# Window attention with channel mix on one core: a new order of 1054 steps, new buffer slots, and 33 steps on other engines

## The chip, the cores and the metric

The kernel runs on one core of a Trainium2 chip. The metric is the device time of one launch in microseconds (us), as the median of several runs. A core has five engines that run side by side and wait for one another by semaphores: TensorE (PE in the profile; its weight loads are a row of their own, PEld), VectorE (DVE), ScalarE (ACT), GpSimd (POOL) and SyncE (SP), which here only issues DMA transfers. ScalarE's queue issues six transfers too. An engine takes its instructions in the order in which the program gives them to it.

## The reference

Attention with a window of 128 positions and four sink positions, over 4 batches, 8 heads, 768 positions and 64 dimensions a head; its output, heads side by side as 512 columns, goes into a channel mix with a squared ReLU.

```python
scores = scale * np.matmul(q, k.transpose(0, 1, 3, 2))
keep = is_sink | in_window                      # positions 0..3, or 0 <= i - j < 128
a = softmax(np.where(keep, scores, -1e9))
x = np.matmul(a, v)                             # to (4, 768, 512)
xk = mu_k * x + (1.0 - mu_k) * x_prev           # x_prev: x one position earlier
xr = mu_r * x + (1.0 - mu_r) * x_prev
k = np.maximum(xk @ w_k, 0.0)                   # 512 -> 1024
v = k * k @ w_v                                 # 1024 -> 512
r = 1.0 / (1.0 + np.exp(-(xr @ w_r)))
return (r * v).astype(np.float32)
```

## The kernel before

The work is cut into 12 units of 256 positions, three to a batch; T is the unit's place in its batch. Units 0 to 11 go through four stages, and several units are under way at a time.

- `prepare`: q, k and v come from memory as f32 (two transfers each, tiles `qs`, `ks`, `vs`). A cast turns each half of q and k into bf16 (`qb`, `kb`, line 540; the profile has lines 529 and 536) and each half of v (`vb`, line 641; 639 in the profile). Then q and k are transposed: for early units on TensorE (line 569) with an evacuation from PSUM into `qt` or `kt` (line 588; 582 in the profile), for k of units 4 to 11 and q of units 8 to 11 by a DMA transpose that SyncE issues (line 555). Once a batch, GpSimd copies the sink keys to `ksink` (line 663) and VectorE makes the sink values `vsink` (line 673).
- `attend`: scores of two pairs of heads (line 714) and of the sinks (line 689), exponentials by ScalarE (lines 768 and 696), the mask by VectorE (line 782), the product with v (lines 756 and 801), and the division by the sum (lines 815 and 818) into `x`.
- `mix`: `x` is transposed on TensorE (line 842), evacuated to `xt` (line 851), or by DMA for units 9 to 11 (line 862); VectorE makes the difference `td` (line 870) and eight tiles of `xk` and `xr` (line 881).
- `ffn`: products of keys (line 932), ReLU (`rl`, line 942 on ScalarE, 946 on VectorE), square (`kk`, line 954), gate (line 963), tanh (`th`, line 969), products of values (line 981; 902 for the last half), the last multiplication (`ob`, lines 990 and 912) and the store (lines 997 and 917).

The program first makes a list of 1054 steps, numbered in the order in which the code writes them. Three tables then decide how they run. `ORDER` is the order in which the steps' instructions are given out; each engine keeps its own steps in this order, so it is the order of every queue. Negative entries are filler products of TensorE on a tile `warm` (line 1001). `SLOTS` says which copy of its buffer each tile gets, in the order of the steps that take one: there are two pairs of PSUM banks for scores (`sc`), four PSUM banks for everything else (`bank`), three to six copies of most tiles in SBUF. `CHOICE` sets the engine of those steps that more than one can do: the casts of q, k and v (540, 641) and of the weights (502), the evacuations (588, 855) and the ReLU (949). A step not named there stays with the engine that the code gives it.

A step that takes a PSUM bank waits until the bank's last user has been read out. A step of ScalarE, VectorE or GpSimd that waits holds up all steps behind it in its queue, and so does a transfer on SyncE's queue that waits for its buffer or its data.

```python
        for i in ORDER:
            if i < 0:
                self.fill(self.pools["bank"][-1 - i])
            else:
                self.ops[i]["emit"]()
```

`BY_ACT = ('v1','v2')` has the loads of v for units 1 and 2 issued by ScalarE's queue; it stands so in both kernels.

Of the kernel before, what the change touches and what calls it, by code (L numbers as in the profile page):

```python
# [18 lines left out]
    90: "ACT", 92: "ACT", 94: "POOL", 95: "ACT", 97: "ACT", 98: "ACT", 100: "DVE", 108: "DVE",  # L19
    111: "DVE", 112: "ACT", 139: "DVE", 142: "POOL", 144: "DVE", 145: "POOL", 151: "ACT", 152:  # L20
    "ACT", 154: "DVE", 161: "DVE", 196: "POOL", 199: "POOL", 204: "DVE", 206: "DVE", 284:
    "POOL", 286: "DVE", 287: "ACT", 288: "ACT", 300: "DVE", 308: "DVE", 356: "POOL", 360: "DVE",
    363: "POOL", 366: "DVE", 367: "ACT", 441: "POOL", 447: "ACT", 449: "DVE", 518: "POOL", 521:
    "POOL", 527: "ACT", 595: "POOL", 602: "POOL", 605: "ACT", 606: "ACT", 677: "DVE", 683:
    "ACT", 684: "ACT", 753: "POOL", 755: "POOL", 761: "DVE", 762: "ACT", 832: "DVE", 834: "DVE",
    838: "DVE", 839: "ACT", 906: "DVE", 914: "ACT", 915: "ACT", 1024: "DVE", 1032: "DVE", 1036:
    "DVE",
# [1028 lines left out]
```

## Time and profile before

| what | us |
|---|---|
| median of 3 runs | 170.99 (169.44 to 171.17) |
| the profiled execution | 170.01 |
| its span, first to last instruction | 168.0 |
| TensorE busy in the span | 159.3 |
| VectorE busy | 150.1 |
| ScalarE busy | 126.4 |
| GpSimd busy | 22.5 |
| DMA moved | 34.61 MB, 206 GB/s |

The granted TensorE clock is 1.00 over the whole span. In the profile a busy TensorE is one with any product under way, each with the time that its pipeline takes; how fast products follow one another is seen from the starts of neighbours.

### The profile page before, as it was taken

What the parts mean: (1) busy time and instruction counts of PE and PEld (TensorE: products, weight loads), DVE (VectorE), ACT (ScalarE), POOL (GpSimd) and SP (SyncE); (2) the same over time, 40 slices, a digit from 0 to 9 for tenths busy, and PEclk for the clock granted to TensorE, in tenths of its full rate; (3) what the DMA queues carried; (4) which work ended last, traced back from release to release, by engine and by line L of the source; (5) the groups of instructions that cost most, each with busy time, mean ns of one, the idle gap of its engine ahead of it and who ended that gap; (6) DMA issues with size and microseconds to landing.
All of it is one profiled execution on the core that took longest, in us unless ns stands there. A gap on an engine that the chain in (4) does not pass through costs nothing.

```text
span 168.0 us, 4214 instructions
## 1 busy us (share of the span) xinstructions
PE 159.3 (95%) x1599; PEld 101.9 (61%) x1599; DVE 150.1 (89%) x384; ACT 126.4 (75%) x207; POOL 22.5 (13%) x48
## 2 busy tenths in 40 slices
PE   7979996999999999999998999999999999999992
PEld 2444575754658576667656668665675576664851
DVE  5079998999999999999999699999999999979962
ACT  3398998999889989878997899998479567532120
POOL 6342002414120414100204000000000000000000
PEclk9999999999999999999999999999999999999999
DMA  5999999999999999699789999899966736133303
GB/s 132 336 305 338 362 239 381 359 314 311 207 257 143 257 266 250 131 220 235 173 192 150 195 247 250 185 247 161 189 154 124 191 80 219 50 48 94 125 0 125
DMA packets 79043, 34.61 MB, mean 206 GB/s; under 512 B 67112, under 2 KB 73520, under 8 KB 79024
## 3 DMA queue, kind: packets, MB, share of 16 engines
q1 hardware_dynamic: 74848, 33.30, 83.4%
q10 hardware_dynamic: 4176, 1.05, 3.1%
q8 instruction: 12, 0.20, 0.6%
q14 instruction: 7, 0.06, 0.1%
HBM read 24.12 MB, written 6.29 MB: 181 GB/s over the span
## 4 chain that ended last, share of the span: by engine, by line
PE 64%; DMA 15%; DVE 9%; ACT 4%; SPq 2%; issue 2%; POOL 1%; ACTq 0%; POOLq 0%
PE bank L932 20%; PE bank L981 19%; PE bank L963 10%; DMA ks<-in_k_dram 9%; DMA vs<-in_v_dram 7%; PE bank L801 5%; PE sc L714 4%; DVE kk L954 2%; DVE e L782 1%; PE bank L842 1%; PE bank L569 1%; PE bank L756 1%; DVE xr L881 1%; SPq L330 1%; PE bank L902 1%
## 5 line engine op out<-in xcount | busy, mean ns | idle before, releaser
L932 PE MATMUL bank<-xk,wk_sb 128*128 128x256 bf16 x384 | 49.2, 273 | 0.3 <-DVE ob L990 0.3
L981 PE MATMUL bank<-wv_h,kk 128*128 128x512 bf16 x184 | 46.4, 379 | 0.0
L768 ACT ACTIVATE e<-sc 128x1024 bf16<-128x1024 f32 (+1 forms) x48 | 44.7, 962 | 1.6 <-PE sc L714 1.4
L932 PEld LDWEIGHTS <-wk_sb 128*128 128x128 bf16 x384 | 35.9, 98 | 9.1 <-issue 0.4
L942 ACT ACTIVATE rl<-bank 128x512 bf16<-128x512 f32 x44 | 25.1, 600 | 14.7 <-PE bank L932 13.8
L782 DVE TENSOR_TENSOR e<-e,mask 128x1024 bf16<-128x1024 bf16 (+1 forms) x48 | 31.3, 658 | 0.0
L981 PEld LDWEIGHTS <-kk 128*128 128x128 bf16 x184 | 16.6, 98 | 15.2 <-DVE kk L954 0.4
L963 PE MATMUL bank<-wr_sb,xr 128*128 128x512 bf16 x96 | 24.0, 379 | 0.3 <-ACT es L696 0.3
L881 DVE SCALAR_TENSOR_TENSOR xk<-td,mu_all,xt 128x256 bf16<-128x256 bf16 x48 | 22.6, 498 | 0.0
L954 DVE TENSOR_TENSOR kk<-rl 128x512 bf16<-128x512 bf16 x48 | 20.7, 446 | 1.5 <-ACT rl L942 1.3
L881 DVE SCALAR_TENSOR_TENSOR xr<-td,mu_all,xt 128x256 bf16<-128x256 bf16 x48 | 22.0, 475 | 0.0
L969 ACT ACTIVATE th<-bank 128x512 f32<-128x512 f32 x24 | 14.2, 610 | 7.4 <-PE bank L963 7.3
L818 DVE TENSOR_TENSOR x<-bank,rec 128x256 bf16<-128x256 f32 x48 | 19.1, 415 | 0.3
L801 PE MATMUL bank<-vb,e 128*128 128x65 bf16 x352 | 17.4, 194 | 0.6 <-DVE e L782 0.3
L990 DVE SCALAR_TENSOR_TENSOR ob<-th,bank 128x512 f32<-128x512 f32 x23 | 15.6, 679 | 2.5 <-issue 1.7
L801 PEld LDWEIGHTS <-e 128*128 128x128 bf16 x352 | 14.2, 97 | 5.0 <-DVE e L782 1.2
L963 PEld LDWEIGHTS <-xr 128*128 128x128 bf16 x96 | 9.1, 98 | 9.2 <-issue 0.3
L714 PE MATMUL sc<-qt,kt 64*128 64x128 bf16 (+1 forms) x256 | 13.8, 237 | 0.1
L1001 PE MATMUL bank<-warm 128*128 128x512 bf16 x42 | 12.4, 433 | 1.1 <-DVE warm L1019 1.1
L639 ACT CAST vb<-vs 128x512 bf16<-128x512 f32 x16 | 10.2, 639 | 1.3 <-DMA vs<-in_v_dram 1.3
L714 PEld LDWEIGHTS <-kt 64*128 64x128 bf16 x256 | 9.2, 94 | 3.3 <-issue 1.7
L870 DVE TENSOR_TENSOR td<-xt 128x512 bf16<-128x512 bf16 x24 | 10.0, 420 | 1.3 <-ACT xt L851 0.8
(71 smaller groups left out, 147.3 us busy)
## 6 DMA issues: line engine op xcount, KB each, us to landing
qs<-in_q_dram SPq DMA_DIRECT2D x24, 256.0 KB, 4.6
ks<-in_k_dram SPq DMA_DIRECT2D x24, 256.0 KB, 4.7
out_dram<-ob SPq DMA_DIRECT2D x23, 256.0 KB, 2.4
vs<-in_v_dram SPq DMA_DIRECT2D x20, 256.0 KB, 3.9
w<-in_moe_w_k_dram SPq DMA_DIRECT2D x2, 1024.0 KB, 10.1
w<-in_moe_w_v_dram SPq DMA_DIRECT2D x2, 1024.0 KB, 8.8
vs<-in_v_dram ACTq DMA_DIRECT2D x4, 256.0 KB, 4.9
w<-in_moe_w_r_dram SPq DMA_DIRECT2D x1, 1024.0 KB, 9.0
```

Source lines behind the costliest of these rows:

```text
L714: nc.tensor.matmul(out=sc[:, a, o0:o1], lhsT=lhs[rows], rhs=rhs[rows], start=u not in BIAS, stop=True, skip_group_check=u in BIAS)
L768: nc.scalar.activation(out=buf[ek][:, :, lo:], in_=buf[sck][:, :, lo:], func=AF.Exp, scale=scale)
L782: nc.vector.tensor_tensor(out=at, in0=at, in1=m, op=ALU.mult)
L801: nc.tensor.matmul(out=o[:, g, a, :], lhsT=e[:, a, e0:e0 + 128], rhs=rhs, start=(T == 0 and i == 0), stop=(i == len(blocks) - 1), skip_gro ...
L818: P.op("DVE", dve(256), lambda ok=ok, rk=rk, c=c: nc.vector.tensor_tensor(out=buf["x", u][:, :, 128 * c:128 * c + 128].rearrange("p g (a d ...
L881: nc.vector.scalar_tensor_tensor(out=buf[key][:, c, :], in0=buf[tk][:, i, :], scalar=mu[w][:, c:c + 1], in1=xt[:, c, t0 - 1:t0 + 255], op0 ...
L932: nc.tensor.matmul(out=ps[:, i, :], lhsT=wk_sb[:, c, 128 * f:128 * f + 128], rhs=xk[:, c, :], start=(c == 0), stop=(c == NC - 1), skip_gro ...
L942: nc.scalar.activation(out=buf[rk], in_=buf[psk].rearrange("p (i t) -> p i t", i=2), func=AF.Relu)
L954: P.op("DVE", dve(512, 0.52), lambda f2=f2, rk=rk: nc.vector.tensor_tensor(out=buf["kk", u][:, 2 * f2:2 * f2 + 2, :], in0=buf[rk], in1=buf ...
L963: nc.tensor.matmul(out=buf[psk], lhsT=buf["xr", u][:, c, 128 * g:128 * g + 128], rhs=wr_sb[:, c, :], start=(c == 0), stop=(c == NC - 1))
L981: nc.tensor.matmul(out=buf[psk], rhs=wv_h[:, f, :], lhsT=buf["kk", u][:, f, 128 * g:128 * g + 128], start=(f == 0), stop=(f == NF - 1))
L990: P.op("DVE", dve(512), lambda psk=psk, tk=tk, bk=bk: nc.vector.scalar_tensor_tensor(out=buf[bk], in0=buf[tk], scalar=1.0, in1=buf[psk], o ...
```

## The change

The list of steps, the transfers and their queues stay as they are. SyncE's queue has the same 128 transfers in the same order; on ScalarE's queue the two transfers of mu change places. New are the order (`ORDER`), the copies (`SLOTS`) and the engine of 33 steps (`CHOICE`). The fillers go from 42 to 40 and stand at other places, all of them now ahead of the first product of keys (before, one came behind it).

The 33 steps, with unit and half in brackets:

| from, to | steps |
|---|---|
| ScalarE to VectorE (7) | evacuations 102 kt(0,0), 105 qt(0,0), 686 xt of unit 7; casts 202 qb(2,1), 600 kb(7,1), 836 qb(10,1); ReLU 1004 of unit 10 |
| GpSimd to VectorE (5) | casts 94 w_r first half, 145 kb(1,1), 205 vb(2,0), 363 qb(4,1), 526 vb(6,0) |
| VectorE to ScalarE (8) | evacuation 154 xt of unit 0; casts 677 qb(8,0), 761 vb(9,0), 832 qb(10,0), 834 kb(10,1), 838 vb(10,0); ReLU 1024 and 1036 of unit 11 |
| GpSimd to ScalarE (6) | casts 441 kb(5,1), 446 vb(5,0), 518 qb(6,0), 602 qb(7,1), 753 kb(9,0), 755 qb(9,0) |
| ScalarE to GpSimd (6) | casts 281 kb(3,1), 367 vb(4,1), 443 qb(5,1), 675 kb(8,0), 683 vb(8,0), 757 kb(9,1) |
| VectorE to GpSimd (1) | cast 906 kb(11,0) |

The diff, cut to the engine table and the first and last rows of the order; the rest of `ORDER` and all of `SLOTS` are replaced in the same way.

```diff
 CHOICE = {
-    90: "ACT", 92: "ACT", 94: "POOL", 95: "ACT", 97: "ACT", 98: "ACT", 100: "DVE", 108: "DVE",
-    111: "DVE", 112: "ACT", 139: "DVE", 142: "POOL", 144: "DVE", 145: "POOL", 151: "ACT", 152:
-    "ACT", 154: "DVE", 161: "DVE", 196: "POOL", 199: "POOL", 204: "DVE", 206: "DVE", 284:
-    "POOL", 286: "DVE", 287: "ACT", 288: "ACT", 300: "DVE", 308: "DVE", 356: "POOL", 360: "DVE",
-    363: "POOL", 366: "DVE", 367: "ACT", 441: "POOL", 447: "ACT", 449: "DVE", 518: "POOL", 521:
-    "POOL", 527: "ACT", 595: "POOL", 602: "POOL", 605: "ACT", 606: "ACT", 677: "DVE", 683:
-    "ACT", 684: "ACT", 753: "POOL", 755: "POOL", 761: "DVE", 762: "ACT", 832: "DVE", 834: "DVE",
-    838: "DVE", 839: "ACT", 906: "DVE", 914: "ACT", 915: "ACT", 1024: "DVE", 1032: "DVE", 1036:
-    "DVE",
+    90: "ACT", 92: "ACT", 95: "ACT", 97: "ACT", 98: "ACT", 100: "DVE", 102: "DVE", 105: "DVE",
+    108: "DVE", 111: "DVE", 112: "ACT", 139: "DVE", 142: "POOL", 144: "DVE", 145: "DVE", 151:
+    "ACT", 152: "ACT", 161: "DVE", 196: "POOL", 199: "POOL", 202: "DVE", 204: "DVE", 205: "DVE",
+    206: "DVE", 281: "POOL", 284: "POOL", 286: "DVE", 287: "ACT", 288: "ACT", 300: "DVE", 308:
+    "DVE", 356: "POOL", 360: "DVE", 363: "DVE", 366: "DVE", 443: "POOL", 446: "ACT", 447: "ACT",
+    449: "DVE", 521: "POOL", 526: "DVE", 527: "ACT", 595: "POOL", 600: "DVE", 605: "ACT", 606:
+    "ACT", 675: "POOL", 684: "ACT", 686: "DVE", 757: "POOL", 761: "ACT", 762: "ACT", 836: "DVE",
+    838: "ACT", 839: "ACT", 906: "POOL", 914: "ACT", 915: "ACT", 1004: "DVE", 1032: "DVE",
 }
 ...
 ORDER = (
-    4, 80, 12, 2, 83, 81, 77, 3, 0, 82, 1, 8, 85, 9, 112, 79, 86, 84, 5, 6, 78, 7, 103, -1, -2,
-    -3, -4, -1, -2, -3, -4, -1, -2, -3, -4, -1, -2, -3, -4, -1, -2, 115, 19, 100, 106, -3, -4,
+    4, 79, 80, 12, 2, 87, 78, 81, 3, 83, 0, 82, 1, 8, 84, 85, 112, 9, 86, -1, -2, -3, -4, -1,
+    -2, -3, -4, -1, -2, -3, -4, -1, -2, 115, 5, 6, 7, 116, 103, 151, 19, 100, 109, 20, -3, -4,
...
-    1040, 1032, 1029, 1038, 1036, 1042, 1033, 1039, 1037, 1041, 1050, 1043, 1046, 1044, 1051,
-    1047, 1045, 1052, 1048, 1053, 1049,
+    1031, 1029, 1036, 1025, 1040, 1032, 1042, 1033, 1041, 1037, 1038, 1043, 1039, 1050, 1044,
+    1046, 1051, 1045, 1047, 1052, 1048, 1053, 1049,
 )
```

152 rows, old and new, of tables (ORDER, SLOTS) are left out of this document.

## The prediction

> **What bounds the kernel now.** I read the page's busy times first, then a table of busy time by stages, then the chain of waits, and last the timeline where the chain leaves TensorE. In the stage table the columns are the stage, its length, busy time of PE, PEld, DVE, ACT and POOL, clock, DMA share and GB/s.
>
> ```profile
> PE 159.3 (95%) x1599; PEld 101.9 (61%) x1599; DVE 150.1 (89%) x384; ACT 126.4 (75%) x207; POOL 22.5 (13%) x48
> ```
>
> ```profile
> 21.00:30.50 9.50, 8.14 (x107) 5.71 (x106) 8.99 (x25) 8.46 (x13) 1.18 (x2) 1.00 1.02 318
> 30.50:43.00 12.50, 12.15 (x120) 7.47 (x117) 12.48 (x30) 12.45 (x21) 4.72 (x4) 1.00 1.14 312
> 43.00:62.00 19.00, 18.70 (x201) 12.56 (x200) 18.92 (x47) 17.60 (x30) 3.02 (x5) 1.00 1.13 226
> 62.00:84.00 22.00, 21.71 (x251) 14.91 (x249) 21.63 (x57) 19.25 (x34) 3.83 (x5) 1.00 0.90 205
> 84.00:126.00 42.00, 41.18 (x440) 27.71 (x439) 39.49 (x104) 35.37 (x60) 2.30 (x5) 1.00 1.04 197
> 126.00:147.00 21.00, 21.00 (x218) 12.94 (x215) 20.25 (x52) 14.30 (x23) 0.00 (x0) 1.00 0.51 133
> 147.00:168.00 21.00, 17.66 (x123) 11.02 (x119) 14.44 (x35) 4.49 (x8) 0.00 (x0) 1.00 0.28 78
> ```
>
> The reader is to see two engines that are full together. From 30.5 to 62 VectorE lacks 0.02 and 0.08 us of being always busy, and TensorE 0.35 and 0.30; ScalarE is full too from 30.5 to 43 (12.45 of 12.50). From 62 on VectorE gets some air, and from 126 to 147 TensorE has no gap at all. So an edit can win only the gaps of TensorE, and it loses whatever it makes VectorE late before 62. The gaps from 21 to 126 are 1.36 + 0.35 + 0.30 + 0.29 + 0.82 = 3.12 us. TensorE's own work is the same but for two fillers.
>
> The chain of waits (start, length, what) gives the prices that I use, since it goes from start to start where instructions of one engine overlap:
>
> ```profile
> 29.39 1.19 DVE xk L881 x3
> 31.37 0.34 DVE vb L639
> 33.48 0.60 DVE rl L946
> 35.75 0.60 DVE wv_h L498
> 83.81 0.52 ACT vb L639
> 155.97 3.49 PE bank L932 x32
> ```
>
> A cast of half a unit's q, k or v costs VectorE 0.34 and ScalarE 0.52, a ReLU or half a weight costs VectorE 0.60. Keys' products follow one another every 0.109 us near the end (3.49 / 32): a TensorE that waits for nothing.
>
> **The change, part by part.** First VectorE up to the second mask of unit 4 (60.88), whose product with v follows. Its timeline near the start and at that mask (start, busy, line, operands, idle before):
>
> ```profile
> 8.59 0.69 DVE L673 TENSOR_TENSOR vsink<-bank,hmask 128x512 bf16<-128x512 f32 x1
> 10.39 0.69 DVE L582 COPY kt<-bank 128x512 bf16<-128x512 bf16 x1 [1.11 <-ACT kt L582]
> 10.99 0.68 DVE L582 COPY qt<-bank 128x512 bf16<-128x512 bf16 x1
> ...
> 60.88 0.68 DVE L782 TENSOR_TENSOR e<-e,mask 128x1024 bf16<-128x1024 bf16 x1
> ```
>
> An evacuation costs it 0.60 (10.39 to 10.99). Up to that point the change gives it 102 and 105 (1.20), the weight half 94 (0.60), and the casts 202, 145, 205 and 363 (4 x 0.34 = 1.36), and takes 154 away, which I price like a cast: 3.16 - 0.34 = +2.82 us. Four things stand against it.
>
> The first is the hole of 1.11 us ahead of 10.39. VectorE stood there until ScalarE had done the other half of kt, and that half is step 102, which with 105 now stands on VectorE itself just there: -1.11.
>
> The second is what GpSimd's casts cost VectorE:
>
> ```profile
> 31.50 1.71 POOL L500 CAST wr_sb<-w 128x1024 bf16<-128x1024 f32 x1 [4.59 <-DMA w<-in_moe_w_r_dram]
> ...
> 56.47 1.90 POOL L639 CAST vb<-vs 128x512 bf16<-128x512 f32 x2 [8.80 <-DMA vs<-in_v_dram]
> ```
>
> ```profile
> 32.33 1.16 DVE L954 TENSOR_TENSOR kk<-rl 128x512 bf16<-128x512 bf16 x1
> ...
> 34.01 0.41 DVE L954 TENSOR_TENSOR kk<-rl 128x512 bf16<-128x512 bf16 x1
> ...
> 57.06 0.83 DVE L881 SCALAR_TENSOR_TENSOR xk<-td,mu_all,xt 128x256 bf16<-128x256 bf16 x1
> 57.81 0.83 DVE L954 TENSOR_TENSOR kk<-rl 128x512 bf16<-128x512 bf16 x1
> ...
> 118.12 0.48 DVE L881 SCALAR_TENSOR_TENSOR xr<-td,mu_all,xt 128x256 bf16<-128x256 bf16 x1
> ```
>
> Beside the cast of w_r a square takes 1.16 in place of 0.41; beside the two casts of v, 446 and 526, a mix takes 0.83 in place of 0.48 and a square 0.83 in place of 0.41. All three casts leave GpSimd: -(0.75 + 0.35 + 0.42) = -1.52. So a cast moved to VectorE is nearly free: 0.34 or 0.60 in its own row, against 0.35 to 0.75 that it took from VectorE before.
>
> The third runs the other way. Three casts come onto GpSimd in this stretch (281, 443, 367), each with a price between 0 and 0.42; no row says what will stand beside them, so I take half of 1.26: +0.63. The Trainium skill ("GPSIMD Engine Reference", section "Key points") says that GpSimd shares its SBUF interfaces with VectorE and contends with VectorE instructions that have two SBUF inputs. The slow square and mix above agree with that, at 0.83 against 0.41 and 0.48. By that rule all three new casts would meet such an instruction, as most of VectorE's are, and the sum below would come out 0.63 us higher, at 170.6.
>
> The fourth is the place of 205:
>
> ```profile
> 26.86 0.38 PE L842 MATMUL bank<-ident,x 128*128 128x128 bf16 x4 [0.76 <-ACT rl L942]
> 27.91 0.38 PE L842 MATMUL bank<-ident,x 128*128 128x128 bf16 x4 [0.45 <-ACT xt L851]
> 30.47 1.20 PE L932 MATMUL bank<-xk,wk_sb 128*128 128x256 bf16 x9
> ```
>
> ```profile
> 27.90 0.43 DVE L870 TENSOR_TENSOR td<-xt 128x512 bf16<-128x512 bf16 x1 [0.45 <-ACT xt L851]
> ```
>
> The td at 27.90 waited 0.45 for ScalarE's xt, and 205 now stands ahead of it: its 0.34 is hidden there. VectorE's account is 2.82 - 1.11 - 1.52 + 0.63 - 0.34 = **+0.48 us**, with ends of -0.15 and +1.11 as the three casts cost 0 or 0.42 each.
>
> The two transposes of x in the same rows show what the new bank copies do. Before, the second one (27.91) took the bank that the first had just filled and waited for its evacuation. Now it takes a bank that VectorE freed earlier, so its 0.45 goes. I cost the gain at nothing: the keys of unit 1 start at 30.47 as the third `xk` of the chain ends (29.39 + 1.19 = 30.58, whose pipeline end is a little later than its release), behind td and so behind ScalarE's xt. What ScalarE waits for there, k of unit 2, comes through the unchanged queue. The two fillers less also stand ahead of that point and are worth nothing.
>
> ScalarE between 30.5 and 43 loses the cast 281, 0.52 us out of a full stage; TensorE's own gap there is 0.35, so the gain lies between 0 and 0.35, and I take the middle: **-0.18**.
>
> The chain leaves TensorE for long only once after 62:
>
> ```profile
> 85.09 5.29 DMA ks<-in_k_dram
> ...
> 90.50 1.04 POOL kb L529
> 91.54 0.34 POOL ksink L663
> ```
>
> ```profile
> 92.53 0.29 PE L689 MATMUL bank<-qt,ksink 128*32 128x256 bf16 x4 [0.82 <-POOL ksink L663]
> ```
>
> GpSimd's queue held `ksink` of unit 6 behind the cast 753 of k of unit 9, which came from memory at 90.4; TensorE then lacked 0.82. In the new kernel 753 is ScalarE's, behind other work there behind the exponentials of unit 7, and `ksink` stands behind 675 (k of unit 8), whose data is older. The wait goes, and what is late next is only TensorE's own queue: **-0.82** (at worst 0, if another engine is as late).
>
> The moves after that change VectorE's load in our favour: of the steps behind 62 us, eight leave it for ScalarE. From 126 on TensorE has no gap to give, so I cost this at nothing, and the three ReLU moves at the end too: ScalarE has 4.49 us of work in the last 21. The cover is thin at one place: 1004, 0.60 on VectorE, now stands ahead of `xk` of unit 11, which the last 32 products of keys need at 155.97. If nothing hides it, it costs up to 0.60.
>
> Sum: +0.48 - 0.18 - 0.82 = -0.52. The profiled execution took 170.01 (span 168.0, 2.0 around it), so its like comes to 169.5. The three runs have a mean of 170.53, 0.5 above the profiled one, and a median of 170.99; with 0.5 added I forecast **170.0 us**. The terms' ends give 170.53 - 0.15 - 0.35 - 0.82 = 169.2 and 170.53 + 1.11 + 0.60 = 172.2.
>
> **The rivals.** *Most of TensorE's gaps close.* The new order and copies remove many waits like the one at 27.91, not one. For it: the 3.12 us of gaps lie at many small places, and ScalarE's queue loses 202 and 281 as well as 102 and 105 in the first 43 us. Against: VectorE is as full as TensorE up to 62, so gaps there can't just be pulled shut. With two thirds of them gone (2.1) it comes to 168.4, with all of them to 167.4.
>
> *VectorE falls behind before 62.* Its +2.82 are sure, what stands against them is not. If the two evacuations don't fill the hole (no -1.11) and GpSimd's remaining casts meet as many squares and mixes as before (no -1.52, and 1.26 for the three new ones), VectorE is 2.82 + 1.26 - 0.34 = 3.74 late at the second mask of unit 4, and TensorE behind it; with the 0.82 of `ksink` kept this is +2.92, or 173.4. Past one per cent it goes when more than 172.70 - 170.53 + 0.82 = 3.0 us come late there. For it: VectorE has 0.10 us of air in 31.5. Against: the hole and the three slow rows are plain.
>
> *SyncE's queue is held up near 113.* Its issues, the median time from issue to landing, and the scores of unit 10:
>
> ```profile
> 111.12 2.25 SPq L555 DMA_TRANSPOSE kt<-kb  x1
> ...
> 116.65 2.50 SPq L555 DMA_TRANSPOSE qt<-qb  x2
> ```
>
> ```profile
> qt<-qb SPq DMA_TRANSPOSE x8, 3.4
> ```
>
> ```profile
> 124.76 0.61 PE L714 MATMUL sc<-qt,kt 64*128 64x256 bf16 x12
> ```
>
> The cast 836 of q of unit 10 goes from ScalarE to VectorE, behind the mix of unit 8 at 118.12 and one td, priced like a cast. With its own 0.34 it is done at 118.12 + 0.40 + 0.34 + 0.34 = 119.2 at the earliest by the old times, 2.5 after the old issue of the transpose, which then lands at 119.2 + 3.4 = 122.6. The scores need it at 124.76, which leaves 2.2 us. Two loads of k of unit 11 and one of v wait in the same queue behind 834, moved behind a tanh of ScalarE. Only if this comes more than 2.2 later still does TensorE wait; at 5 later it would cost 2.8 and give 170.0 + 2.8 = 172.8.
>
> **How the numbers follow.** One per cent of the median, about what a measurement of this kernel can tell from no change, puts the marks at 169.28 and 172.70. The forecast has a chance of 0.46, the closing of the gaps 0.31 (its times lie below the lower mark), VectorE's lateness 0.14 and SyncE's 0.09 (both counted above the upper mark). So faster 0.31, same 0.46, slower 0.23. The range takes in the forecast's ends and most of both neighbours: 167.5 to 173.0, with perhaps 0.08 below and 0.11 above. The likeliest case's own range is 169.2 to 172.2.
>
> **What would show it.** VectorE without the idle microsecond ahead of 10.39, and at the second mask of unit 4 within a microsecond of its old 60.88; no square of 1.16 near 32; the sink scores of unit 7 without a wait; the stage from 30.5 to 43 no emptier on TensorE. I am wrong if TensorE shows new gaps over half a microsecond after 30, above all ones ended by `e` of line 782, or if the keys of unit 1 start far from 30.5.

## The result, and the profile after

| | kernel before | changed kernel |
|---|---|---|
| median of 20 runs each | 170.81 us (168.97 to 172.51) | 168.63 us (167.99 to 170.84) |
| ratio, 95% interval | | 0.9903 [0.9876, 0.9931] |
| repeated later, 17 and 12 runs | 170.46 us | 169.15 us, ratio 0.9943 [0.9911, 0.9975] |
| profiled execution, span | 170.01, 168.0 us | 169.03, 167.0 us |
| second profiled execution, span | 171.43, 169.4 us | 167.96, 165.9 us |

The ratios leave disturbed runs out. The change makes the kernel 0.6 to 1.0% faster by these two comparisons (their intervals reach from 0.25 to 1.24%). The two medians of the first comparison lie 2.2 us apart and the two profiled executions only 1.0: the one of before lay low among its runs, that of the changed kernel high among its own. With the second pair it is the other way round: 171.43 lies 0.4 to 1.5 above every median of before on record, and 167.96 is the shortest of its twelve. Both pairs are read here.

The busy times and stages of the changed kernel, in the columns of the prediction (its lines carry numbers lower by one):

```profile
PE 157.9 (95%) x1578; PEld 101.9 (61%) x1597; DVE 149.4 (89%) x387; ACT 127.7 (76%) x208; POOL 16.9 (10%) x44
```

```profile
21.00:30.50 9.50, 8.28 (x104) 5.63 (x103) 8.38 (x22) 7.88 (x13) 0.75 (x1) 1.00 1.10 349
30.50:43.00 12.50, 11.88 (x117) 7.64 (x118) 12.50 (x31) 11.96 (x20) 2.24 (x3) 1.00 1.04 294
43.00:62.00 19.00, 18.77 (x193) 12.53 (x194) 18.93 (x49) 17.80 (x32) 1.62 (x4) 1.00 0.93 212
62.00:84.00 22.00, 21.84 (x259) 15.14 (x261) 21.64 (x60) 20.97 (x37) 2.14 (x5) 1.00 0.94 211
84.00:126.00 42.00, 41.63 (x435) 27.89 (x441) 39.32 (x103) 37.27 (x64) 3.25 (x5) 1.00 1.09 202
126.00:147.00 21.00, 20.84 (x221) 13.53 (x224) 19.86 (x52) 12.50 (x19) 0.00 (x0) 1.00 0.49 132
147.00:167.00 20.00, 16.67 (x105) 10.20 (x105) 13.39 (x31) 5.16 (x9) 0.00 (x0) 1.00 0.24 79
```

The two engines are as full together as before; from 84 to 126 TensorE has 0.45 us more under way, and that is the largest change of TensorE that this table shows. (The trace lacks 19 records of products; the 1597 weight loads are complete.) The timelines say more. VectorE near the start, at 22 to 24 us and at the second mask of unit 4, and TensorE at the sink scores of unit 7:

```profile
8.81 0.68 DVE L581 COPY qt<-bank 128x512 bf16<-128x512 bf16 x1
9.41 0.68 DVE L581 COPY kt<-bank 128x512 bf16<-128x512 bf16 x1
10.01 0.68 DVE L581 COPY qt<-bank 128x512 bf16<-128x512 bf16 x1
...
23.82 0.69 DVE L499 CAST wk_sb<-w 128x1024 bf16<-128x1024 f32 x1 [1.12 <-DMA w<-in_moe_w_k_dram]
...
61.04 0.69 DVE L781 TENSOR_TENSOR e<-e,mask 128x1024 bf16<-128x1024 bf16 x1
```

```profile
90.37 0.29 PE L688 MATMUL bank<-qt,ksink 128*32 128x256 bf16 x4
```

The hole of 1.11 us near 10 is closed, evacuation follows evacuation at 0.60. A new wait of 1.12 us for w_k stands at 22.7. The sink scores of unit 7 carry no wait. The same places in the second trace of the changed kernel:

```profile
22.24 0.69 DVE L499 CAST wk_sb<-w 128x1024 bf16<-128x1024 f32 x1
...
59.96 0.69 DVE L781 TENSOR_TENSOR e<-e,mask 128x1024 bf16<-128x1024 bf16 x1
```

There the wait for w_k is missing, and the mask and the keys of unit 1 come 1.1 and 1.35 us earlier.

To put all traces on one scale, TensorE's time from the first product of keys of unit 1 to the start of the fourth last product of the kernel (the last one starts 0.33 us later in each trace) is split in two. *Work* is an estimate of what its products take when nothing holds them, 126.85 us, made from the intervals between starts in the trace of before and the same for every version. *Waits* is the rest, so that only the differences between its rows count. Then end = keys of unit 1 + 126.85 + waits.

```
trace                              keys of unit 1   waits      end
before                                      30.47    6.74   164.06
before, second trace                        32.93    5.71   165.50
before, ksink first                         31.82    5.46   164.13
before, fillers                             30.47    6.47   163.79
before, fillers and ksink first             30.54    6.29   163.69
changed                                     30.74    5.59   163.18
changed, second trace                       29.39    5.87   162.11
changed, three casts back on GpSimd         29.75    6.75   163.35
changed, w_v late                           29.45    5.72   162.02
changed, v issued later                     32.35    5.96   165.16
new order, old engines, mu early            32.28    8.54   167.68
new order, old engines                      34.23    9.02   170.11
old order, new engines                      32.30    9.75   168.91
```

The kernel before and its versions (with the old engines) reach the keys of unit 1 at 30.5 to 32.9, the changed kernel at 29.4 to 30.7; behind that point the waits go from 5.5 to 6.7 down to 5.6 to 5.9. Where the gain is won, the two pairs say differently: in the first the changed kernel's head (all that is ahead of the keys of unit 1) is 0.27 us later and its waits are 1.15 less, in the second its head is 3.54 earlier and its waits 0.16 more. So how the gain divides between the head and the rest is not shown. Two rows are not typical of their versions: the traced execution of the new order with the old engines took 175.62 us, that with mu early 173.19, which is 2.7 and 2.3 above their medians.

### The profile page after: what moved, and what is told of

It is laid out like the page before. It is cut to its first block, busy times and chain, and to the rows that moved or that the text cites. A ratio compares the mean times of both kernels' runs of the same rounds, so it can differ in the third digit from the quotient of the medians.

```text
span 167.0 us, 4192 instructions
## 1 busy us (share of the span) xinstructions
PE 157.9 (95%) x1578; PEld 101.9 (61%) x1597; DVE 149.4 (89%) x387; ACT 127.7 (76%) x208; POOL 16.9 (10%) x44
## 4 chain that ended last, share of the span: by engine, by line
PE 75%; DMA 13%; DVE 6%; issue 2%; ACT 1%; SPq 1%; ACTq 0%
PE bank L980 23%; PE bank L931 22%; PE bank L962 12%; DMA w<-in_moe_w_k_dram 8%; PE bank L800 6%; PE sc L713 5%; DMA qs<-in_q_dram 3%; DMA vs<-in_v_dram 2%; PE bank L841 2%; PE bank L568 1%; DVE xk L880 1%; PE bank L755 1%; PE bank L901 1%; DVE x L817 1%; PE bank L688 1%
## 5 line engine op out<-in xcount | busy, mean ns | idle before, releaser
L931 PE MATMUL bank<-xk,wk_sb 128*128 128x256 bf16 x384 | 49.7, 273 | 1.3 <-DVE wk_sb L499 0.6
L980 PE MATMUL bank<-wv_h,kk 128*128 128x512 bf16 x173 | 45.2, 379 | 0.5
L931 PEld LDWEIGHTS <-wk_sb 128*128 128x128 bf16 x384 | 35.8, 98 | 10.3 <-DVE wk_sb L499 0.9
L941 ACT ACTIVATE rl<-bank 128x512 bf16<-128x512 f32 x45 | 26.1, 602 | 11.9 <-PE bank L931 10.6
L781 DVE TENSOR_TENSOR e<-e,mask 128x1024 bf16<-128x1024 bf16 (+1 forms) x48 | 30.6, 646 | 0.3 <-ACT e L767 0.2
L880 DVE SCALAR_TENSOR_TENSOR xk<-td,mu_all,xt 128x256 bf16<-128x256 bf16 x48 | 21.6, 476 | 0.1
L953 DVE TENSOR_TENSOR kk<-rl 128x512 bf16<-128x512 bf16 x48 | 19.8, 429 | 1.0 <-ACT rl L941 0.9
```

The source lines that it names most:

```text
L781: nc.vector.tensor_tensor(out=at, in0=at, in1=m, op=ALU.mult)
L880: nc.vector.scalar_tensor_tensor(out=buf[key][:, c, :], in0=buf[tk][:, i, :], scalar=mu[w][:, c:c + 1], in1=xt[:, c, t0 - 1:t0 + 255], op0 ...
L931: nc.tensor.matmul(out=ps[:, i, :], lhsT=wk_sb[:, c, 128 * f:128 * f + 128], rhs=xk[:, c, :], start=(c == 0), stop=(c == NC - 1), skip_gro ...
L941: nc.scalar.activation(out=buf[rk], in_=buf[psk].rearrange("p (i t) -> p i t", i=2), func=AF.Relu)
L953: P.op("DVE", dve(512, 0.52), lambda f2=f2, rk=rk: nc.vector.tensor_tensor(out=buf["kk", u][:, 2 * f2:2 * f2 + 2, :], in0=buf[rk], in1=buf ...
L980: nc.tensor.matmul(out=buf[psk], rhs=wv_h[:, f, :], lhsT=buf["kk", u][:, f, 128 * g:128 * g + 128], start=(f == 0), stop=(f == NF - 1))
```

## The experiments

**1. ksink ahead of the cast.** In the kernel before, one entry of the order moves on GpSimd's queue.

```diff
-    57, 594, 606, 753, 622, 528, 633,
+    57, 594, 606, 528, 753, 622, 633,
```

> The kernel before, with one step moved: on GpSimd's queue the copy of ksink (528) goes ahead of the cast of k of unit 9 (753), which waits for a DMA until about 90.4 us; nothing else is changed. Theory of the prediction (the wait of the sink scores of unit 7 at 92.53 us is worth its own length): that wait of 0.82 us is gone and all that comes after is earlier by as much, so 0.8 us less in the median, a ratio near 0.995. Rival (there is slack behind it, as the following products find VectorE and ScalarE no further on): the wait goes, but waits of the same sum appear between 93 and 126 us, and the ratio is 1.000.

Measured: 169.59 us, ratio 0.9945 [0.9911, 0.9979]. TensorE at the place where the prediction showed 0.82 us of waiting:

```profile
92.01 0.60 PE L930 MATMUL bank<-xk,wk_sb 128*128 128x256 bf16 x4
92.54 0.29 PE L687 MATMUL bank<-qt,ksink 128*32 128x256 bf16 x4
```

The wait is gone. This execution reached the keys of unit 1 at 31.82, 1.35 later than the first trace of before, and ends only 0.07 later, since its waits are 5.46 and not 6.74. The median fits the price of 0.8 (the interval takes in 0.4 to 1.5 us); run 9 does not. The trace doesn't decide it: in the second trace of before, with ksink still behind the cast, a late head leaves waits of 5.71 too, and the wait for ksink is smaller there:

```profile
93.96 0.29 PE L689 MATMUL bank<-qt,ksink 128*32 128x256 bf16 x4 [0.30 <-POOL ksink L663]
```

**2. Other transfers ahead, in the kernel before.** Meant to change only which completion the second half of k of unit 2 waits for.

```diff
-    83, 81, 77, 3,
+    83, 81, 3,
...
-    116, 88, 109, 105, 10,
+    116, 77, 88, 109, 105, 13, 10,
...
-    113, 111, 13, 117,
+    113, 111, 117,
```

> The kernel before, with two transfers issued at other places of ScalarE's queue (mu of k two instructions later, the second half of v of unit 1 three earlier), so that the second half of k of unit 2 on SyncE's queue has to wait for the completion of k of unit 1 and no longer for that of v of unit 1 (20.8 us). It should then be issued near 13 us instead of 20.8, and the second part of w_v near 14 instead of 21.5. Theory A: the head is bound by VectorE's account and not by these loads, so no change, 0.998 to 1.002. Theory B: the hold of SyncE's queue was part of what the kernel before lost ahead of the keys of unit 1 (30.5 us), so 0.4 to 1 us less, 0.994 to 0.998. Theory C: loads that start together slow the ones that are needed first (w_k landed 2.8 us later in the changed kernel), so 0.3 to 1 us more.

Measured: 173.51 us, 1.0202 [1.0158, 1.0245]. None of the three theories. TensorE shows why:

```profile
7.98 0.39 PE L567 MATMUL bank<-ident,qb 128*128 128x128 bf16 x4
11.82 0.27 PE L477 MATMUL bank<-ident,ob 8*128 8x8 f32 x1 [3.46 <-DMA ob<-in_moe_mu_k_dram]
```

The small product that transposes mu stands early in TensorE's queue. The 2 KB of mu_k, issued at 8.4 instead of 1.3, let the whole queue stand for 3.46 us. The experiment changed something other than it meant to, and says nothing on the completions.

**3 and 4. Engines alone, order alone.** The changed kernel's `CHOICE` in the old order and copies, and the reverse.

```diff
 CHOICE = ...                  # 3: the changed kernel's;  4: as before
 ORDER = ...; SLOTS = ...      # 3: as before;  4: the changed kernel's
```

> The changed kernel's choice of engines in the order (and banks) of the kernel before. By the terms of the prediction without those that come from the order: VectorE +2.82 us up to the second mask of unit 4, collisions -1.52, three casts newly on GpSimd +0.63 (94, 446 and 526 off GpSimd stay gone), and the idle hole ahead of 10.39 and the wait for ksink as before, except that 753 now is ScalarE's and ksink no longer stands behind a cast on GpSimd, so -0.82: in all about +1 us, 1.003 to 1.010. Rival (the engines bring the gain by themselves and the order little): 0.990 to 0.995.

> The changed kernel's order (and banks) with the choice of engines of the kernel before. By the terms that come from the order alone: the idle hole of VectorE ahead of 10.39 us filled, -1.11 on VectorE's account, and ksink ahead of the cast of k of unit 9, -0.82; the collisions with GpSimd's casts of w_r and of units 5 and 6 stay. So -0.8 us (ksink alone) to -1.9 us (both), 0.989 to 0.995. Rival (order and engines only work together, because each queue's order was made for its engine's load): 1.003 or more.

Measured: engines alone 174.66 us, 1.0230 [1.0172, 1.0287]; order alone 172.88 us, 1.0173 [1.0125, 1.0220]. For the engines alone both ranges were missed; for the order alone the rival's holds. The parts don't add: each by itself costs 2.3 or 1.7%, and together they gain 0.6 to 1.0%. In the table both have 9 to 9.75 us of waits behind the keys of unit 1, where old with old and new with new have 5.5 to 6.8 (the order alone in an untypical execution). No run says why the engines alone are slow. With the order alone TensorE also loses time in the head, at mu again:

```profile
11.44 0.39 PE L1001 MATMUL bank<-warm 128*128 128x512 bf16 x1
13.87 0.24 PE L479 MATMUL bank<-ident,ob 8*128 8x8 f32 x1 [2.04 <-issue]
```

ScalarE's queue then, where the transfer of mu_k stands behind an evacuation that the changed kernel gives to VectorE:

```profile
9.35 0.58 ACT L582 COPY qt<-bank 128x512 bf16<-128x512 bf16 x1 [0.93 <-PE bank L569]
9.36 0.26 ACTq L367 DMA_DIRECT2D ob<-in_moe_mu_k_dram  x1
```

In the changed kernel the same transfer goes out at 7.01.

**5. Order alone, with mu early.**

```diff
-    4, 79, 80, 12, 2, 87, 78, 81,
+    4, 79, 80, 12, 2, 87, 78, 77, 81,
...
-    104, 101, 105, 77, 110,
+    104, 101, 105, 110,
```

> The changed kernel's order and banks with the choice of engines of the kernel before, as in e4, but with the transfer of mu_k (2 KB, on ScalarE's queue) issued near 2 us instead of 9.4. In e4 TensorE stood 2.2 us at 11.44 ahead of the small product that needs mu, its clock was granted at 0.84 between 10 and 21 us, and the keys of unit 0 came at 25.23 us, 4 us late. Theory (a late mu is what makes the new order slow with the old engines): the keys of unit 0 come near 21.2 again and most of the 1.7% goes, 0.993 to 1.002. Rival (the two parts only fit together, with the loss spread over the kernel): 1.008 or more, with the gaps of e4 at 100 and 104 us still there.

Measured: 170.90 us, 1.0052 [1.0021, 1.0083]. Between the two ranges. Mu explains 1.2 of the 1.7%, and the keys of unit 0 come at 21.09 as expected. The waits behind the keys of unit 1 are 8.54 in this trace, as the rival has it, but its execution took 2.3 us more than the median, so how much of them usually stays is not shown.

**6. v of unit 1 issued later, in the changed kernel.**

```diff
-    148, 117, 13, 108, 123, -2, 88, 143, 113, 149, 144, 118, 114,
+    148, 117, 108, 123, -2, 88, 143, 113, 149, 144, 118, 13, 114,
```

> The changed kernel with one step moved: the second half of v of unit 1 is issued two instructions later on ScalarE's queue, so that the second half of k of unit 2 on SyncE's queue again waits for its completion, as in the kernel before; mu is where it was. SyncE's queue should then stand from about 13 to 20 us, and w_v come late as before. Theory A (prediction's account: the head is bound by VectorE): no change, ratio to the kernel before 0.988 to 0.993. Theory B (the loads together slow w_k, and the wait of 1.1 us of VectorE at 22.7 us with 0.78 us on TensorE goes): 0.3 to 0.8 us less than the changed kernel, 0.984 to 0.989. Theory C (k of unit 2 late costs the keys of unit 1): 0.3 to 1 us more, 0.993 to 0.997.

Measured: 170.84 us, 1.0063 [1.0029, 1.0096], 1.2 to 1.6% above the changed kernel, worse than the worst theory. ScalarE, with its queue's own transfers (ACTq):

```profile
19.71 0.59 ACT L579 COPY qt<-bank 128x512 bf16<-128x512 bf16 x1
23.30 0.62 ACT L636 CAST vb<-vs 128x512 bf16<-128x512 f32 x1 [3.00 <-DMA vs<-in_v_dram]
```

SyncE's queue did stand 10.3 us as foreseen, but k of unit 2 was not what anybody waited for: from 24 to 62 us no wait of TensorE, VectorE or ScalarE ends with it, nor with w_r or w_v, which came late too. ScalarE stood 3.00 us at its own cast of v of unit 1, and the ReLUs behind it held TensorE. The second trace of the kernel before has the same wait, the first has 0.29 at this place, the changed kernel none:

```profile
20.29 0.42 ACT L696 ACTIVATE es<-bank 128x256 bf16<-128x256 f32 x1
22.41 0.62 ACT L639 CAST vb<-vs 128x512 bf16<-128x512 f32 x1 [1.71 <-DMA vs<-in_v_dram]
```

```profile
19.09 0.59 ACT L581 COPY qt<-bank 128x512 bf16<-128x512 bf16 x1
19.56 0.64 ACT L638 CAST vb<-vs 128x512 bf16<-128x512 f32 x1
```

(The last two are the second trace of the changed kernel.) All traces together show what goes with it, the race of two issues near 10 us: the second half of v of unit 1 on ScalarE's queue against the first megabyte of w_k on SyncE's.

```
trace                       v issued   w_k issued   behind by   v's packets in its best us   wait at the cast
before, mu late (run 2)         8.76        10.79       -2.03                          826          -
changed, casts back             9.68         9.96       -0.28                          662          -
before, fillers + ksink        10.17        10.34       -0.17                          626          -
before                          9.83         9.97       -0.14                          727       0.29
changed, w_v late               9.82         9.95       -0.13                          703          -
changed, second trace           9.84         9.91       -0.07                          785          -
changed                         9.99        10.05       -0.06                          621          -
engines alone                   9.99        10.00       -0.01                          695          -
before, ksink first             9.95         9.82       +0.13                          720       0.16
order alone                     9.90         9.77       +0.13                          705          -
before, fillers                 9.94         9.79       +0.15                          695          -
order alone, mu early          10.27         9.91       +0.36                          170       1.99
before, second trace           10.13         9.60       +0.53                          165       1.71
changed, v later               11.26        10.15       +1.11                          163       3.00
```

(The best microsecond is the one with the most packets among the first four of the transfer.) Ahead of w_k, or up to 0.15 us behind it, v moves 620 to 830 packets in its best microsecond; 0.36 behind and later it gets at most 170. The order alone stands between: 145 and 163 packets in its first two microseconds, 705 in the third. Only runs 2 and 6 move the issue of v by an edit of its own; the other differences come with other edits or from one execution to the next. In the second trace of before, from 15 to 19 us, the two queues move 158, 165, 155, 149 packets of v and 159, 164, 153, 152 of w_k in each microsecond: one for one, but a packet of w_k has 2048 bytes and one of v 256. The Trainium skill ("DMA: Bandwidth & Descriptors", section "Queues, rings and completion order") says that each DMA engine takes turns between its queues, a whole packet at a time; the equal counts agree with taking turns. Of the seven traces with the old order six have a wait for v of 0.3 us or less, so the long one is not the usual one.

**7. Three casts back on GpSimd, in the changed kernel.**

```diff
+    94: "POOL", 446: "POOL", 526: "POOL",
-    446: "ACT", 526: "DVE",
```

> The changed kernel with three casts back on GpSimd: w_r (94), v of unit 5 (446), v of unit 6 (526). VectorE is spared 0.60 + 0.34 us, ScalarE 0.53; by the prediction GpSimd's casts then slow VectorE's squares and mixes beside them by 0.75 + 0.35 + 0.42 = 1.52 us, so +0.6 us on VectorE's account and 0.2 to 0.6 us more than the changed kernel, ratio to the kernel before 0.991 to 0.994, and the profile should show at least two instructions of VectorE that take 0.35 us or more over their kind beside these casts. Rival (the collisions depend on where the cast happens to fall and cost nothing here): 0.5 to 0.9 us less than the changed kernel, 0.984 to 0.988.

Measured: 168.87 us, 0.9932 [0.9905, 0.9960], inside the expected range, though not told apart from the changed kernel's repeats (0.9903, 0.9943). The trace shows the expected slow instructions, a mix beside the cast of w_r and a difference beside that of v, 1.27 for 0.48 and 0.83 for 0.42. That they cost the kernel time is not shown.

```profile
31.52 1.27 DVE L881 SCALAR_TENSOR_TENSOR xr<-td,mu_all,xt 128x256 bf16<-128x256 bf16 x1
...
56.70 0.83 DVE L870 TENSOR_TENSOR td<-xt 128x512 bf16<-128x512 bf16 x1
```

**Second trace of the kernel before.**

> The kernel before once more, for a second trace. Its profiled run took 170.01 us, the median of its runs is 170.8. Theory (the head differs from run to run): the keys of unit 1 come at 30.5 us in one and up to 1.3 us later in the other, as in the trace of the first experiment (31.82 us, with a granted clock of 0.88 between 21 and 30.5), and from 31 us on the two are alike within 0.2 us. Rival (it differs in many small steps over the whole kernel): the keys of unit 1 within 0.3 us and the difference spread.

Measured: 171.43 us, keys of unit 1 at 32.93. The head does differ, by 2.47 us, more than the theory's 1.3: besides ScalarE's wait of 1.71 us, TensorE's clock falls. The stage table from 26 to 33 us (clock in the third column from the end):

```profile
26.00:28.00 2.00, 0.93 (x23) 0.73 (x21) 1.75 (x7) 1.79 (x3) 1.16 (x2) 1.00 0.97 355
28.00:29.00 1.00, 0.55 (x10) 0.43 (x8) 0.34 (x2) 0.74 (x2) 0.00 (x0) 1.00 0.82 209
29.00:30.00 1.00, 0.90 (x10) 0.71 (x9) 1.00 (x4) 0.91 (x2) 0.00 (x0) 0.68 0.85 315
30.00:31.00 1.00, 1.00 (x8) 0.46 (x8) 1.00 (x4) 0.59 (x1) 0.00 (x0) 0.50 1.03 397
31.00:32.00 1.00, 1.00 (x14) 0.68 (x11) 1.00 (x4) 0.59 (x1) 0.00 (x0) 0.50 1.05 393
32.00:33.00 1.00, 1.00 (x9) 0.39 (x8) 1.00 (x3) 1.00 (x2) 0.21 (x1) 0.61 1.05 406
```

TensorE's products from 29.39 to the keys of unit 1 at 32.93 take 1.47 us more than the same ones in the first trace (28.40 to 30.47). What comes later isn't alike within 0.2 us, as the theory had it: the late head gives 1.03 us of its waits back (5.71 for 6.74).

**8 and 9. Fillers in the gaps, without and with ksink first.** In the kernel before, six more products that nobody reads.

```diff
-    190, 27, 207, 205, 194, 186, 208, 187, 191, 195, 192, 166, 214,
+    190, 27, -2, -2, -2, -2, 207, 205, 194, 186, 208, 187, 191, 195, 192, 166, -4, -4, 214,
```

> The kernel before with six more filler products on TensorE (products of zeros that nobody reads, 0.22 us each), four ahead of the first transpose of x of unit 1, two ahead of the second, in the gaps of 0.93 and 0.62 us at 25.7 and 27.1 us; the rest is as before. Theory (the clock): in two further traces of this head (the first experiment and the repeat) TensorE's granted clock falls to 0.50 for some 3 us right behind these gaps, and three steps at 28.7 to 32 us take 1.6 us more; in the first trace it didn't fall. If little use of TensorE in the gaps is what brings it down, the fillers hold it at 1.00, and the median falls by 0.7 to 1.5 us, ratio 0.991 to 0.996, with fewer long runs. Rival (the clock falls for another reason, or the fillers only delay what follows): 0.999 to 1.004, and the clock falls again or the keys of unit 1 come no earlier than 31.5 us.

> The kernel before with both edits, the six filler products of e8 and ksink ahead of the cast of k of unit 9 as in the first experiment (0.9945 by itself). Theory (the gain of the change is these two, the wait for ksink and the clock that falls in most runs of the head before): the product of the two, 0.986 to 0.991, as fast as the changed kernel with its 0.9903. Rival (what the change gained came from the engines or from ScalarE's wait for v of unit 1): it stays at 0.993 to 0.996, slower than the changed kernel.

Measured: 169.75 us, 0.9998 [0.9965, 1.0030], and 169.78 us, 1.0009 [0.9981, 1.0037]. The clock stays at 1.00, and the longest of their runs take 170.5 and 170.8 where those of before took 173.3. But the typical time doesn't move, as the rival of run 8 has it. Of 91 runs of the kernel before, 8 had a mean clock under 0.995, among them four of the six over 172 us. So the fall goes with long runs and doesn't explain the median; and with 8 in 91, none in these 24 runs may be chance, so that the fillers hold the clock is not shown. Nor does ksink first bring anything here: with the fillers alone the sink scores came only 0.25 us later behind the products ahead of them than in run 9 (0.78 for 0.53), with a wait of 0.19 that the profile puts down to an evacuation, while the copy of ksink ends 0.05 us ahead of them:

```profile
92.25 0.29 PE L687 MATMUL bank<-qt,ksink 128*32 128x256 bf16 x4 [0.19 <-ACT xt L849]
```

In run 9 TensorE waited longer at another place, for VectorE (0.5 us with the fillers alone):

```profile
42.40 0.42 PE L799 MATMUL bank<-vb,e 128*128 128x65 bf16 x8 [0.76 <-DVE e L780]
```

The theory of run 9, that the two edits are the gain of the change, falls; its rival's range, 0.993 to 0.996, is missed too.

**10. w_v late, in the changed kernel.**

```diff
-    226, 16, 227, 174, 184, 233, 14, 92,
+    226, 227, 174, 184, 233, 14, 16, 92,
```

> The changed kernel with the transfer of the second half of w_v put behind that of w_r on SyncE's queue, so that it is issued near 22 us and no longer at 13.7, beside w_k, k of unit 2 and v of unit 1. Theory (the loads beside it make w_k late): the second half of w_k lands before 22.7 us, VectorE's wait of 1.1 us for it and 0.78 us of TensorE at 23.4 us go, the keys of unit 1 come 0.3 to 0.8 us earlier than at 30.74, and so does the end: ratio to the kernel before 0.985 to 0.989. Rival 1 (VectorE's account up to 30 us is full, so the time is only moved to another wait): as the changed kernel, 0.989 to 0.992. Rival 2 (w_v then comes too late for its first cast at 32.5 us and holds ScalarE): 0.993 or more.

Measured: 168.28 us, 0.9909 [0.9878, 0.9941], in the range of rival 1; its profiled execution has a span of 165.8 us, VectorE's wait for w_k is gone, and the keys of unit 1 come at 29.45.

**Second trace of the changed kernel.**

> The changed kernel once more, for a second trace and beside the last experiment (168.28 us with w_v late). Theory (the head of the changed kernel is earlier and steadier than that of the kernel before, and its first trace was one of its later ones): keys of unit 1 between 29.5 and 30.8 us, waits of TensorE behind them of 5.4 to 5.8 us in sum as in its first trace (5.59, against 6.74 and 5.71 before), no fall of the clock between 21 and 31 us, ratio 0.988 to 0.993, and a median 0.1 to 0.7 us above that of the kernel with w_v late. Rival (the wait for w_k varies from run to run and w_v late gains nothing): the median within 0.1 us of 168.28, and no wait of VectorE for w_k in this trace.

Measured: 169.15 us, 0.9943 [0.9911, 0.9975]. This trace has the keys of unit 1 at 29.39 and no wait for w_k either, without the edit of run 10: the two traces end within 0.1 us of one another. So the wait comes and goes, as the rival says, and the head of 29.45 is no proof for the edit. The theory's ranges are narrowly missed (keys 29.39 for 29.5, waits 5.87 for 5.8, ratio 0.9943 for 0.993). The medians (168.28 beside 170.08 before, 169.15 beside 170.46) leave a gain of some 0.3% possible and don't show it. No version is shown to beat the changed kernel.

## Why the prediction was right or wrong

The time was forecast at 170.0 with 167.5 to 173.0; it is 168.6. The likeliest case had 0.3% less, measured are 0.6 to 1.0% less. On the forecast's base of 170.53 that is 169.6 and 168.9, on both sides of the mark of 169.28 below which the prediction put the times of its rival with the closed gaps. So the direction is right and the size too small, and the stated range took the time in because it was wide enough for three cases. By its steps:

- **VectorE up to the second mask of unit 4, +0.48: this step failed.** VectorE's account from its first cast of k to that mask, in three traces:

```
trace                    starts    idle   start to start   mask at
before                     8.24    1.85            50.78     60.88
changed                    8.47    1.41            51.16     61.04
changed, second trace      8.31    0.77            50.88     59.96
```

  Its own work (start to start) was to grow by 2.82, less 1.52 for the collisions that go, plus 0.63 for new ones, 1.93 in all; it grew by 0.38 and 0.10. The steps that VectorE gained and lost do cost their 2.82. Of what is missing, 0.69 is a step that I overlooked: `vsink` (116), which stood behind the first cast of k before, stands ahead of it now. The sixteen reciprocals of line 815 take 0.3 to 0.4 less in sum, for a reason that no run shows.

  The rest is the collisions, mis-sized. I counted three and overlooked a fourth cast that leaves GpSimd: beside 145 the mask at 12.81 took 0.93 in place of 0.55. Up to the second mask of unit 4 seven instructions of VectorE took at least 0.1 us over the median of their kind beside GpSimd's casts before, 2.82 us in sum; in the changed kernel five took 1.54, in its second trace four took 1.25. And this differs between executions: in the second trace of before five took 1.80, and the square near the cast of w_r, which ScalarE's ReLU held until 34.14, took 0.42. Of the three new casts only 367 cost about its 0.42 (0.35 and 0.32); 443 met nothing, and 281 cost at most 0.07.

  That the mask comes 0.16 us later in the first trace, near the forecast's 0.48, is luck: the own work grew by 1.55 less than forecast, and the idle time fell by 0.44 in place of 1.45. In the second trace the mask comes 0.92 earlier.
- **The hole ahead of 10.39, -1.11: right**, it is gone in both traces. What was missing is the wait for w_k that took its place in one of the two.
- **The keys of unit 1 wait for ScalarE's xt, so that the bank copies win nothing; "what ScalarE waits for there, k of unit 2, comes through the unchanged queue": wrong in its reason.** The queue's order is unchanged, its times are not. What ScalarE waits for at length there is v of unit 1 on its own queue, by 0.3 us in the trace that I read and 1.7 in the next. Six of seven traces of the old order have no more than 0.3, so this wait isn't shown to be what the change usually wins.
- **ScalarE from 30.5 to 43, -0.18: not separated by any run.** In the first trace the stage is emptier on TensorE (11.88 busy for 12.15), against the sign that I named; in the second it is fuller (12.38). A gap of just over half a microsecond, ended by `xk`, has come behind the keys of unit 1 in both, of the kind that I said would prove me wrong, and still the waits behind these keys are hardly longer than before (5.59 and 5.87 for 6.74 and 5.71). The first and the second trace of the changed kernel:

```profile
31.52 1.14 PE L931 MATMUL bank<-xk,wk_sb 128*128 128x256 bf16 x9 [0.51 <-DVE xk L880]
```

```profile
30.18 1.03 PE L931 MATMUL bank<-xk,wk_sb 128*128 128x256 bf16 x8 [0.52 <-DVE xk L880]
```

- **ksink, -0.82: right in mechanism, too sure in size.** Its wait is gone. By itself the edit gave 0.5% (run 1), on top of the fillers nothing (run 9). The wait was 0.82 us in the trace that I read, 0.30 in the second and 0.19 with the fillers; I took the largest for its size.
- **The end, 0: right.** Behind the sink scores of unit 7 TensorE's waits are 1.92 us before, 2.10 and 2.11 after; 1004 cost at most these 0.2 us, and no wait of TensorE behind 88 us shows in the list of waits of the changed kernel, so SyncE's queue near 113 held nobody.
- **Rivals:** VectorE did not fall behind. Gaps did close in the first pair of traces, 6.74 to 5.59 us behind the keys of unit 1, though not two thirds of them; in the second pair they did not. That the change could fail half-made was no rival of mine, and runs 3 to 5 show it.

Shown by runs that move them is that a late mu and a late v of unit 1 cost time, and that order and engines need one another. That ksink moves the time is open, since runs 1 and 9 disagree; the collisions are seen in the traces, but run 7 doesn't tell their price from nothing. Which of all this makes the gain of 0.6 to 1.0% stays open: the heads of single executions differ by more than the gain. A version of the kernel before in which v of unit 1 is surely issued ahead of w_k, with mu left early, was not tried.

## What to carry to other kernels

Before a wait in a trace is priced, take a second trace, and see where both executions lie among their runs: a wait of 0.3 us on a transfer was 1.7 in the next execution, one of 0.82 was 0.30. Two queues whose issues lie within a few tenths of a microsecond are a race here: 0.36 us behind, the small transfer moved packet for packet with the large one. So issue the small one clearly first. An order made for one placement of work on engines should not be judged, or reused, with another: here the halves of the change alone cost 2.3 and 1.7%.

## What the hardware showed beyond that

- In the second trace of before TensorE's granted clock fell after a stretch in which products were under way for 1.48 of 3 us, with no gap over 1.07 us. At half clock the lack in its four rows (0.32 + 0.50 + 0.50 + 0.39) makes 3.4 us. In the first trace, with 1.74 of 3 us, it did not fall, nor in run 6 after 2.8 us without any product. The first trace at the same place:

```profile
25.00:27.00 2.00, 1.19 (x23) 0.86 (x24) 1.93 (x8) 1.56 (x3) 1.18 (x2) 1.00 1.04 373
27.00:28.00 1.00, 0.55 (x10) 0.43 (x9) 0.56 (x3) 0.72 (x2) 0.00 (x0) 1.00 1.04 391
```

  The Trainium skill ("TensorE: Matmul & The Clock Gate", Part 1) has the clock halved after an idle window of some 3.4 us, and the windows run freely, whatever the kernel does. The length of the fall and its coming and going agree; that the window must be idle does not. How much use keeps the clock up, these runs don't show.
- An instruction of VectorE that collides with a cast on GpSimd waits for the end of the cast. In the trace of before, casts that ended at 33.21, 40.64, 57.61 and 58.36 were followed by the ends of three squares and a mix at 33.49, 40.92, 57.89 and 58.64, 0.28 us later each time, though the casts had taken 0.66 to 1.71 us; masks end 0.41 or 0.54 behind theirs, by their size. So a collision costs what is left of the cast when VectorE's instruction starts, and neither the kind of cast nor that of the instruction alone prices it.
- In this program each transfer carries one of eight completion semaphores (16 or 17 of the 134 transfers each), handed out in turn over both queues, and isn't issued until the last transfer with the same one has landed. In the kernel before, k of unit 2 on SyncE's queue so waited for v of unit 1 on ScalarE's, and all behind it: in three traces it was issued 0.02 us after v had landed (at 20.80, 22.41 and, in run 6, 23.29). SyncE's waits from 9 to 25 us, before:

```profile
SPq L330 <- DMA vs<-in_v_dram: 8.3, 1, 8.3
```

  In the two traces of the changed kernel SyncE waits for v 0.3 and 0.4 us in this stretch, though its queue is the same: the new order of the steps had given v another semaphore.
